# Order of the first loads and of batch 0's small steps in a windowed attention and ResMLP kernel

## Chip, cores and metric

The kernel runs on one core of a Trainium2 chip. The metric is the device time of one execution in microseconds (us). An execution has five engines: TensorE (PE, matmuls), VectorE (DVE), ScalarE (ACT), GpSimd (POOL) and SyncE (SP, which here only issues DMAs). Each works through its own instructions in the order in which they are given.

## The reference

Two stages in a row, with B = 4 batches, H = 8 heads, S = 768 positions, D = 64, d_model = H x D = 512 and d_ff = 2048:

```python
scores = q @ k.T / sqrt(D)                       # per batch and head
keep = (pos_k < 4) | ((pos_q - pos_k >= 0) & (pos_q - pos_k < 128))
a = softmax(where(keep, scores, -1e9))           # 4 sink keys and a window of 128
x = concat_heads(a @ v)                          # (B, S, 512)

a1 = alpha1 * x + beta1                          # ResMLP, affine in place of a norm
u = x + lam * (w_tok @ a1)                       # mixes the 768 positions
a2 = alpha2 * u + beta2
out = u + lam * (relu(a2 @ w_ch1) @ w_ch2)
```

Inputs and the output are float32; the matmuls of the kernel work in float16 with float32 sums.

## The kernel before

Positions are cut in six blocks of 128 rows. For a pair of heads (hp 0 to 3) and t = 0 (q) or 1 (k), `load_qk` fetches a tile, `trans` turns it with six or twelve PE transposes against the identity `iden` (L509, L512) and copies the result from PSUM to `qkT` (the evacuation, task name `ev`). For each key block j, `scores` (L617, L622), or for the first half of the heads of batch 0 `scores_by_pair` (L683, L686), makes scores in PSUM, ACT takes the exponential into `E`, and masking is done either by adding a bias tile with a matmul (`bias0`, `biasn`, L617, L683) or by a multiplication afterwards (`mk`). `sinks` and `fill_vs` handle the four sink keys (`ks`, `vs`, with the selector `sel` and the block mask `bm`). `pv` multiplies with v (L716, L723); DVE divides by the sums (L748, L749) into `x`; `half` (L758) forms the scaled copy `xh` on POOL. `tok` (L854) mixes positions with `wtokT`, the transposed w_tok, whose rows `cast_wtok` casts and transposes (L814). `uTp` (L895) transposes u, `mlp1` (L934) and `mlp2` or `prod` (L1119, L1051) are the channel MLP.

In batch 0 the first pair of heads is loaded as float32 from SyncE (`nat`, L402) and cast to float16 by DVE (L157). The six tiles of the other pairs are cast on the way by loads that GpSimd asks for (`CASTING`, L395, tile `n`). SyncE also asks for v (L429, twelve pieces), w_tok (L440, six row blocks), then for w_ch2 (`load_w`, L449) and the later batches. GpSimd asks for w_ch1 in four quarters (L453), which the 16 units fi of `mlp1` need in fours: fi 0 to 3 the first, fi 12 to 15 the fourth. Small DMAs (`gate`, L460) make SyncE wait until a quarter has landed before it asks for more.

Every step is a task, numbered in the order of the calls of `add`. `emit` writes the tasks out by four tables: `ORDER` (the order of all, and so of each engine), `ENGINES` (which engine does task i), `HOMES` (which physical buffer each tile has) and `IDLES`: (i, home, n) puts n matmuls of 128 x 128 on zeros ahead of task i on PE. These fillers (L148) keep PE occupied; nothing reads them.

A tile in the home of an earlier tile waits for that one's last reader. In before, q's float16 tile follows w_tok's first block in one `n16` home, and the last casting load takes the `nat` home of k's float32 tile. The masks (`make_masks`, L338 to L346), the selector (`make_sel`, L370, with the small identity `iden8`), the block mask (`make_bm`, L359) and `iden` (`make_iden`, L330) are made on POOL out of tiles that DVE has filled; `make_bias` (L353) makes the bias tiles of the masks on DVE.

## Time and profile before

| | |
|---|---|
| time, median of 3 runs | 255.96 us (254.75 to 256.95) |
| profiled execution, its own time | 255.43 us |
| span of its instructions | 253.2 us |
| PE busy | 245.4 us (97%) |
| DVE busy | 190.7 us (75%) |
| ACT busy | 133.3 us (53%) |
| POOL busy | 102.2 us (40%) |
| PE's clock granted | 1.00 throughout |
| DMA moved | 38.79 MB |

The span runs from the first to the last instruction; the profiled execution took 2.2 us more than its span. Busy times are sums over an engine's instructions. Times in the timelines count from the span's start. The name out<-in says which tile an instruction writes and which it reads, with the numbers of the buffers left out.

### The profile page before, as it was taken

To read this page: it belongs to the slowest core of one execution; us is meant where nothing else is said; L and a number is where in the kernel's file an instruction comes from. 1 tells how busy PE (TensorE), PEld (TensorE's weight loads), DVE (VectorE), ACT (ScalarE), POOL (GpSimd) and SP (SyncE) were. 2 spreads that over 40 slices of the span, in tenths; PEclk is the share of its full clock that TensorE was granted. 3 is DMA by queue.
4 is the path that set the end of the run, shared out by engine and by line. 5 is a ranking of instruction groups with operands and counts; after the bars stand their busy time and mean duration, and the time that the engine had idled before them with its cause. 6 is when DMAs were issued, how large, how long until landed. Compare 5 with 4: busy or idle time off the path is not lost.

```text
span 253.2 us, 5499 instructions
## 1 busy us (share of the span) xinstructions
PE 245.4 (97%) x2167; PEld 159.8 (63%) x2167; DVE 190.7 (75%) x402; ACT 133.3 (53%) x219; POOL 102.2 (40%) x124
## 2 busy tenths in 40 slices
PE   8699999999999999999999999999999999999993
PEld 7555646676545544566687686567677676667882
DVE  5588987877788874978879986577778983228892
ACT  2499925879976034787932535566660235543000
POOL 8317854895247417525682040065562220000010
PEclk9999999999999999999999999999999999999999
DMA  6999999999979998997485674420000140100317
GB/s 170 207 240 292 229 276 311 330 362 285 221 130 250 247 194 158 192 244 168 107 176 117 114 151 124 132 66 0 3 0 3 38 83 7 41 0 3 122 70 268
DMA packets 86129, 38.79 MB, mean 153 GB/s; under 512 B 73540, under 2 KB 80460, under 8 KB 86104
## 3 DMA queue, kind: packets, MB, share of 16 engines
q1 hardware_dynamic: 66576, 28.06, 46.9%
q10 hardware_dynamic: 15784, 7.11, 11.9%
q0 software_dynamic: 3744, 3.28, 8.3%
q8 instruction: 17, 0.28, 0.5%
q14 instruction: 8, 0.07, 0.1%
HBM read 29.91 MB, written 6.29 MB: 143 GB/s over the span
## 4 chain that ended last, share of the span: by engine, by line
PE 94%; DMA 3%; DVE 0%; SPq 0%; issue 0%
PE h L934 33%; PE P L1051 22%; PE tok L854 12%; PE ch L1119 8%; PE pv L723 5%; PE S L622 4%; DMA nat<-in_k_dram 3%; PE S L617 2%; PE tp L512 1%; PE pv L716 1%; PE tp L509 1%; PE wT L814 1%; PE sk L554 1%; PE idle L148 1%; PE uTp L895 1%; PE pv L609 1%
## 5 line engine op out<-in xcount | busy, mean ns | idle before, releaser
L934 PE MATMUL h<-uT,w1f 128*128 128x384 f16 x512 | 89.6, 327 | 0.0
L934 PEld LDWEIGHTS <-w1f 128*128 128x128 f16 x512 | 48.2, 98 | 31.0 <-issue 1.7
L940 ACT ACTIVATE hT<-h 128x384 f16<-128x384 f32 x77 | 37.0, 491 | 38.0 <-PE h L934 37.9
L1051 PEld LDWEIGHTS <-hT 128*128 128x128 f16 x408 | 39.4, 98 | 6.8 <-issue 0.2
L942 DVE TENSOR_SCALAR hT<-h 128x384 f16<-128x384 f32 x51 | 27.8, 555 | 20.3 <-PE h L934 19.6
L644 ACT ACTIVATE E<-S 128x1024 f16<-128x1024 f32 (+1 forms) x39 | 38.1, 1002 | 8.1 <-PE S L622 6.6
L767 POOL TENSOR_TENSOR tm<-x,la_b 128x512 f32<-128x512 f32 x18 | 24.3, 1350 | 25.2 <-DVE x L749 13.4
L854 PE MATMUL tok<-xh,wtokT 128*128 128x512 f16 x144 | 33.0, 379 | 0.0
L1064 DVE TENSOR_TENSOR x<-x,P 128x256 f32<-128x256 f32 x45 | 18.3, 419 | 11.3 <-PE P L1051 10.2
L1051 PE MATMUL P<-w2f,hT 128*128 128x256 f16 x216 | 26.5, 273 | 0.0
L854 PEld LDWEIGHTS <-wtokT 128*128 128x128 f16 x144 | 13.9, 98 | 15.0
L1119 PE MATMUL ch<-w2f,hT 128*128 128x512 f16 x96 | 23.2, 380 | 0.0
L1051 PE MATMUL P<-w2s,hT 128*128 128x256 f16 x192 | 23.1, 273 | 0.0
L1087 POOL TENSOR_TENSOR x<-x,pt 128x256 f32<-128x256 f32 x4 | 3.4, 855 | 47.5 <-DVE pt L1082 47.5
L155 ACT CAST u<-x 128x512 f16<-128x512 f32 x15 | 9.2, 615 | 24.9 <-DVE x L861 24.3
L749 DVE TENSOR_TENSOR x<-pv,rec 128x256 f32<-128x256 f32 x48 | 20.4, 425 | 1.7
L155 ACT CAST n<-nat 128x768 f16<-128x768 f32 x21 | 16.9, 828 | 7.4 <-DVE x L1130 6.3
L723 PEld LDWEIGHTS <-E 128*128 128x128 f16 x328 | 14.8, 97 | 5.0 <-issue 1.3
L861 DVE TENSOR_TENSOR x<-x,tok 128x512 f32<-128x512 f32 x24 | 16.0, 683 | 2.4 <-PE tok L854 2.3
L723 PE MATMUL pv<-vfs,E 128*128 128x65 f16 x328 | 17.6, 194 | 0.0
L584 POOL TENSOR_SCALAR_AFFINE_SELECT E<-E 128x512 f16<-128x512 f16 x12 | 7.5, 646 | 21.1 <-ACT E L644 21.1
L748 DVE RECIPROCAL rec<-pv 128x4 f32<-128x4 f32 x48 | 8.6, 179 | 7.7 <-PE pv L723 7.1
(134 smaller groups left out, 339.9 us busy)
## 6 DMA issues: line engine op xcount, KB each, us to landing
wst_w<-in_moe_w_ch_dram SPq DMA_DIRECT2D x8, 512.0 KB, 8.3
nat<-in_q_dram SPq DMA_DIRECT2D x10, 384.0 KB, 4.1
vnat<-in_v_dram SPq DMA_DIRECT2D x14, 256.0 KB, 5.4
nat<-in_k_dram SPq DMA_DIRECT2D x8, 384.0 KB, 6.6
out_dram<-x SPq DMA_DIRECT2D x11, 256.0 KB, 3.1
out_dram<-x ACTq DMA_DIRECT2D x10, 256.0 KB, 3.8
wtn<-in_moe_w_tok_dram SPq DMA_DIRECT2D x6, 384.0 KB, 4.5
w1f<-in_moe_w_ch_dram POOLq DMA_DIRECT2D x4, 512.0 KB, 14.0
```

Source lines behind the costliest of these rows:

```text
L155: nc.scalar.copy(o, i)
L644: nc.scalar.activation(eT.t, pS.t[:, :, 0 : n * w].rearrange("p e (i w) -> p e i w", i=n), AF.Exp, scale=scale)
L723: nc.tensor.matmul(po.t[:, hl, :], eT.t[:, e_, off + i, c : c + P], vf[j][:, h, :], start=(r < 2 and n == 0), stop=(n == len(parts) - 1 an ...
L749: nc.vector.tensor_mul(bx.t[:, 4 * G : 4 * G + 4, :], po.t[:, :, 0:D], rec.t.to_broadcast([P, 4, D]))
L767: engine[e].tensor_mul(bt.t, bx.t.rearrange("p h d -> p (h d)"), la1_b)
L854: nc.tensor.matmul(pt.t, wtokT[:, si, ti * P : (ti + 1) * P], hs[si].t, start=(si == 0), stop=(si == NR - 1))
L934: nc.tensor.matmul(ph.t, w1f[:, c, fi * P : (fi + 1) * P], bu.t[:, c, chk * NTOK : (chk + 1) * NTOK], start=(c == 0), stop=(c == NC - 1))
L940: nc.scalar.activation(bh.t[:, fi, :], ph.t, AF.Relu)
L942: nc.vector.tensor_scalar_max(bh.t[:, fi, :], ph.t, 0.0)
L1051: nc.tensor.matmul(pc.t, hh[:, nt * P : (nt + 1) * P], w(fi), start=(first and n_ == 0), stop=(n_ == HF - 1), skip_group_check=True)
L1064: nc.vector.tensor_add(row(bx)[:, cols], row(bx)[:, cols], pc.t)
L1119: nc.tensor.matmul(pc.t, bh.t[:, fi, nt * P : (nt + 1) * P], w2f[:, fi, :], start=(fi == 0), stop=(fi == NF - 1))
```

## The change

Only the four tables change. Of the first instructions of each engine, before and after (numbers are tasks):

| engine | before | after |
|---|---|---|
| SP | w_tok block 0 (26), q (6), k (7), then v | q (6), k (7), w_tok block 0 (26), then v; all the rest as before |
| POOL | casting load (9), sel and iden8 (5), loads 8 and 15, masks (1), load 12, bm (3), iden (0), loads 14 and 13, v casts 63 and 65, xh product 115, w_ch1 (32 to 35), xh products | sel and iden8 (5), bm (3), loads 9, 8, 15, 12, iden (0), masks (1), loads 14 and 13, a1 product (39), v cast 65, xh products 115, 118, 130, 127, v cast 66, w_ch1 (32 to 35), xh products |
| DVE | cast of w_tok block 0 (72), vs (4), make_bias (2), q cast (45), k cast (48), a1 (39, 40), b1 (41), ... | vs (4), q cast (45), k cast (48), make_bias (2), evacuation of k (50), b1 (41, 42), evacuation 54, ... |
| ACT | w_tok's evacuation (74), evacuations of q (47) and k (50), exp (91), ... | evacuation of q (47), cast of w_tok block 0 (72), exps (91, 104), evacuation 52, ... |
| PE | 65 fillers, w_tok block 0 (73), 12 fillers, q (46), 1 filler, k (49), 53, 10 fillers, scores 90, 95, ... | 67 fillers, q (46), k (49), 25 fillers, scores 90, 103, transposes 53, 51, scores 95, w_tok block 0 (73), ... |

Tasks 53 and 51 are the transposes of the second pair's k and q, whose loads are 9 and 8. On PE the first `mlp1` units are fi 1, 11, 8, 4, 10, 5 before and 11, 1, 8, 4, 10, 5 after; then, before, one `uTp`, fi 15, the other `uTp`; after, both `uTp` and then fi 15. Later on PE only neighbours change places.

28 of 1143 tasks change their engine, nearly all in batches 0 and 1 (evacuations, casts of w_tok and v, a few of relu and u). Homes: the eight q and k tiles of batch 0 now have eight `nat` homes of their own, q's `n16` home comes ahead of w_tok's block, the two v tiles of heads 4 to 7 have `wst` homes 0 and 1 (before 1 and 3), so that w_ch2's first tile (home 3) no longer follows one of them.

```diff
     ORDER = (
-        26, 6, 9, 7, 10, 5, 11, 8, 18, 15, 72, 19, 1, 12, 3, 0, 4, 2, 22, 14, 73, 74, 45,
-        48, 46, 17, 39, 49, 47, 53, 13, 40, 50, 41, 90, 95, 43, 91, 51, 54, 103, 52, 16, 44,
+        6, 7, 5, 26, 10, 3, 11, 9, 18, 8, 19, 4, 22, 15, 17, 45, 12, 48, 0, 1, 46, 49, 16,
+        28, 14, 2, 50, 47, 13, 72, 21, 39, 41, 90, 103, 20, 91, 42, 53, 104, 51, 54, 24, 95,
...
     HOMES = (
-        "471305760131011000102123203130202001333101040201500112130053316501813134100210a010022031"
+        "145602370010122001202310203211210302203140101100511203013044205121821000203331a501103130"
...
     IDLES = (
-        (73, 0, 65), (46, 0, 12), (49, 1, 1), (90, 3, 10), (61, 3, 2), (109, 3, 3), (92, 3,
-        1), (166, 1, 4), (162, 0, 1),
+        (46, 0, 67), (90, 1, 25), (166, 1, 4), (162, 0, 1),
     )
```

## The prediction

> **What bounds the kernel now.** I read the page's slices first, then the chain of waits in order of time, then the timelines of GpSimd (POOL), VectorE (DVE) and TensorE (PE) over the first 46 us, and last the tile view of `w1f`.

> From the page, three engines in 40 slices of 6.3 us:

> ```profile
> PE   8699999999999999999999999999999999999993
> ...
> POOL 8317854895247417525682040065562220000010
> ...
> DMA  6999999999979998997485674420000140100317
> ```

> PE is full from the third slice to the last. No other engine is. The DMA engines are full for the first eleven slices, so what is asked for first lands first. The chain of waits, its beginning (start, duration, what):

> ```profile
> 1.72 7.97 DMA nat<-in_k_dram
> ...
> 9.71 0.57 DVE n L157
> ...
> 10.33 0.51 PE tp L512 x6
> 10.84 0.46 PE tp L509 x12
> 11.30 0.67 PE idle L148 x10
> 11.96 0.33 PE S L686 x4
> ```

> From 10.33 the chain runs almost wholly through PE, to 248.97; one DVE add and the last store follow. So the end is 10.33 plus PE's work, and what stands ahead of it is the load of batch 0's first k: issued at 1.72, landed at 9.69, cast, transposed. PE also runs fillers (L148, matmuls nobody reads): 77 before its first transpose of q, 22 after it. From 11.96 on, eleven of them are in the stream.

> POOL and DVE, in time (start, duration, engine, operation, idle before and its releaser):

> ```profile
> 2.31 0.54 POOL L370 TENSOR_SCALAR_AFFINE_SELECT sel<-sel 128x128 f16<-128x128 f16 x1
> ...
> 5.42 0.39 POOL L346 TENSOR_SCALAR_AFFINE_SELECT mask<-mask 128x256 f16<-128x256 f16 x1
> ...
> 7.22 0.30 POOL L331 TENSOR_SCALAR_AFFINE_SELECT iden<-iden 128x128 f16<-128x128 f16 x1
> ...
> 10.58 0.71 POOL L395 DMA_DIRECT2D n<-in_k_dram  x1 [2.40 <-DVE n L157]
> ...
> 21.32 3.04 POOL L453 DMA_DIRECT2D w1f<-in_moe_w_ch_dram  x4
> ```

> ```profile
> 7.12 0.22 DVE L353 TENSOR_SCALAR bias<-mask 128x256 f16<-128x256 f16 x1
> 7.25 0.35 DVE L353 TENSOR_SCALAR biasn<-maskn 128x256 f16<-128x256 f16 x1
> 8.11 0.56 DVE L157 CAST n<-nat 128x768 f16<-128x768 f32 x1 [0.51 <-PE wT L814]
> 9.71 0.56 DVE L157 CAST n<-nat 128x768 f16<-128x768 f32 x1 [1.05 <-DMA nat<-in_k_dram]
> ```

> Three things to see: the identity is ready only at 7.52; q, landed at 5.33, is cast at 8.11 because its n16 buffer was the one of w_tok's first block (released by wT); the sixth casting load waits 2.40 for k's cast, since it shares k's nat buffer.

> Last, the place with least slack later, the tile view of `w1f` and PE's timeline:

> ```profile
> L453 POOL DMA_DIRECT2D w1f<-in_moe_w_ch_dram x4: 747/765/812, 21.3 to 23.6; - x4
> DMA to landing us min/median/max: 8.6/14.0/20.9
> ```

> ```profile
> 44.30 0.50 PE L895 MATMUL uTp<-iden,u 128*128 128x128 f16 x6
> 44.63 0.81 PE L934 MATMUL h<-uT,w1f 128*128 128x384 f16 x4
> ```

> The fourth quarter of w_ch1 lands at 23.59 + 20.92 = 44.5, and its first reader (fi 15) starts at 44.63 to 44.80. It has a margin of 0.3.

> [...] q took 4.1 from issue to landing, k, asked for 0.45 later and overlapped by GpSimd's loads, 8.0. [...] one late operand holds everything behind it, as both 8.11 and 10.58 show. [...] The granted clock is 1.00 in every window here, and PE's longest gap is 1.37 (6.20 to 7.57); the new order makes none longer. [...]

> **The change, part by part.**

> *SyncE's queue.* q takes w_tok's slot (issued 0.81, landed 3.2 later: 4.0), k takes q's (1.27 + 4.1 = 5.3, against 9.69). GpSimd's casting loads, the other traffic, start about 1.7 later, so these slots should be no slower. w_tok's block follows; its transposes sit eighth on PE now, at about 11.5. No buffer holds the casts: q at 4.1 to 4.7, k at 5.3 to 5.9. That is 4.4 gained on the data, but it is no longer the latest.

> *GpSimd.* sel needs DVE's memset (ends 1.76) and starts at 1.85 instead of 2.31. By before's start-to-start steps: sel 0.49, its small identity 0.14, bm 0.50, so 3.0; four DMA issues (0.90, 0.75, 0.72, 0.72 in before) to 6.1; identity 0.55, ready at 6.6; masks 1.40 (4.41 to 5.81 in before), ready at 8.0, 2.2 later than before; fifth and sixth load at 8.0 and 8.7, no longer at 7.47 and 10.58. [...] I take 0.2.

> *What is late next.* 67 fillers at 5.15/65 each end at 6.4; the q and k transposes run from 6.7 to 7.6. ACT evacuates q (0.80). k's evacuation goes to DVE, behind make_bias, which waits for the masks: 8.2 [...], bias 0.48, copy 0.96, ready at 9.6. The 25 fillers (0.067 each, 1.7) lie inside this wait and cost nothing. First scores at 9.7 against 11.96.

> *PE's ledger.* Before: 248.97 - 11.96 = 237.0. Leave out 11 fillers (0.74); add the first GpSimd head's transposes (0.46), w_tok's first transposes (0.34, formerly under the wait for k) and 5 fillers (0.33): 237.4. With no wait PE ends at 9.7 + 237.4 = 247.1, a gain of 1.9.

> *Waits that appear.* The second casting load (landed 11.25 in before) is wanted at 9.7 + 0.17 + 0.66 + 0.46 = 11.0. Its issue ends 1.0 later, but q and k no longer share the engines with it: estimated landing 10.6 to 11.6, cost 0 to 0.6, taken 0.2. S of block 4 needs both new evacuations (ACT after two exps, DVE after the b1 fold): 0.2. Later casting loads were 1.0 to 1.9 early in before and are wanted 1.3 to 1.7 earlier: nothing if landings stay. DVE gains about 1.2 of work net from 10 to 32 and had some 2.6 idle there: hidden. ACT loses some. Sum: 1.9 - 0.4 = 1.5.

> *w_ch1.* Its loads move on POOL from behind one xh product to behind four (0.73 each) and a v cast (0.9): by the norms that feed them, issued at about 22.6 instead of 21.3. PE meanwhile wants fi 15 at 44.8 - 1.5 + 0.34 (both uTp now stand ahead) = 43.6. In before nothing of the SyncE queue moved from 26 to 30 because w_ch2's first load waited for the v cast on its buffer; now it doesn't wait and shares from the start. The bytes ahead of the fourth quarter are the same and the engines full, so I take 43.0 to 44.5 for its landing: 0 to 0.9, taken 0. The remaining engine swaps exchange equals beside a full PE: nothing.

> Profiled execution: 255.43 (span 253.2, 2.2 around it) less 1.5 is 253.9. That run lies 0.5 under the median of the runs shown; on the median's scale 255.96 - 1.5 = 254.5.

> **Rivals.** (1) *No wait takes its place.* For it: DMA slots seen, no buffer left shared, 2.6 of DVE idle. [...] 0.72 an issue put the masks at 7.7, first scores at 9.2: ledger gain 2.4, and run scatter of 0.3 or a wait of before that modelled matmul ends hid does the rest: 253.2. Against it: DVE's order is rigid. (2) *The casting loads inherit their later issue.* If the second lands 1.6 later, 12.9, PE waits 1.9 at its transposes, where 0.2 is in the sum: the gain of 1.5 is gone, 256.2. Against it: the first six loads are bound by bandwidth, not issue. (3) *w_ch1 comes late, and the end is slower.* Place: fi 15 on PE. Break-even is a landing at 44.80 + 0.34 = 45.1, 0.6 later than before; each us beyond is one lost. If the landing moves with the issue (1.3) it is 45.8, slower by 0.7; if POOL is also held by the third v block of heads 4 to 7 (landed 20.7 in before) until 23.8, they are issued at 24.7, the last lands at 48, and the run takes 258.8. [...]

> **How the numbers follow.** Forecast 0.37 (254.5, its own range 253.4 to 255.5); rival 1 0.33; rival 2 0.12; rival 3 0.18. One per cent, 2.6 us, is about what a measurement here can tell from no change. Faster by more: rival 1 and 0.05 of the forecast, 0.38. Slower by more: rival 3 and a little of 2, 0.19. Within: 0.43. The range takes in rival 1 and the lighter half of rival 3: 252.6 to 257.8.

> **What would show it.** Right: k cast by 6.0; identity at 6.6 and masks near 8; k's evacuation on DVE starting right after make_bias; first scores at 9.2 to 9.8; 25 fillers ended before that; PE without a gap over 0.5 up to 44; fi 15 at 43 to 44. Wrong: k landing after 7, PE idle at L509 (rival 2), POOL idle ahead of w1f or PE idle at L934 (rival 3), first scores before 9.

## The result, and the profile after

| | before | after |
|---|---|---|
| time, median of 4 runs each | 255.91 us (254.75 to 256.95) | 264.34 us (263.91 to 264.55) |
| profiled execution, its own time | 255.43 us | 264.17 us |
| span | 253.2 us | 261.9 us |
| mean granted clock of PE | 1.000 | 0.985 |

The ratio after to before is 1.0328, 95% interval 1.0282 to 1.0375: slower by 8.4 us, where 1.5 us of gain were forecast. In after's profile every line number is one lower than in before's.

The page of after, the same slices as before:

```profile
PE   8799991999999999999999999999999999999993
...
POOL 7627900694996652625669004043745040000010
PEclk9999997799999999999999999999999999999999
DMA  6999999949995999799763955601000051100217
```

One slice of PE, the seventh (39.3 to 45.8), is nearly empty, and the granted clock falls in that slice and the next. Before had neither. The chain of waits in order of time (start, duration, what) has a DMA in that place:

```profile
31.34 3.47 PE tok L853 x16
38.06 6.21 DMA nat<-in_q_dram
46.17 5.45 PE h L933 x24
```

A load of batch 1's q ends the wait of batch 0's MLP, which doesn't read it. (`uT` is u transposed, taken out of PSUM and scaled by ACT and DVE; these are the "uT scalings" below, and the first `mlp1` matmul, h, reads them.) The waits from 38 to 50 us (who waited for whom: us in total, times, longest) lead there step by step:

```profile
DVE uT L879 <- ACT uT L877: 7.1, 1, 7.1
ACT uT L877 <- DMA nat<-in_q_dram: 7.0, 1, 7.0
PE h L933 <- DVE uT L879: 6.1, 1, 6.1
```

The timeline of the same place (start, duration, engine; the suffix q marks an engine's issuing of DMAs):

```profile
36.66 0.80 SPq L459 DMA_DIRECT2D gates<-w1f  x1
36.76 1.22 ACT L155 CAST u<-x 128x512 f16<-128x512 f32 x2 [0.64 <-DVE x L860]
...
38.06 0.40 SPq L401 DMA_DIRECT2D nat<-in_q_dram  x1
...
41.29 3.45 ACTq L401 DMA_DIRECT2D nat<-in_k_dram  x2
44.94 1.23 ACT L877 ACTIVATE uT<-uTp,ab 128x384 f16<-128x384 f16 x2 [6.97 <-DMA nat<-in_q_dram]
...
45.65 1.04 DVE L879 TENSOR_SCALAR uT<-uTp,ab 128x384 f16<-128x384 f16 x2 [7.11 <-ACT uT L877]
46.17 4.14 PE L933 MATMUL h<-uT,w1f 128*128 128x384 f16 x16 [6.06 <-DVE uT L879]
```

ACT in before, at the same place:

```profile
37.44 0.41 ACTq L402 DMA_DIRECT2D nat<-in_k_dram  x1
39.11 1.38 ACT L878 ACTIVATE uT<-uTp,ab 128x384 f16<-128x384 f16 x2 [1.11 <-PE uTp L895]
...
41.80 0.40 ACTq L402 DMA_DIRECT2D nat<-in_k_dram  x1
```

In after, ACT ends its casts of u at 37.98. Next in its order are two DMA issues, tasks 177 and 171 (batch 1's k of head pairs 3 and 0), and only then the scalings of uT. In before's order 177 stood behind the first cast of u and was issued at 37.44 without a wait; 171 stood behind the scalings, a relu and a cast of u and was issued at 41.80. By the trace's semaphore events, SP's and ACT's 140 transfers share eight semaphores, in before as in after, and none of the 132 issues that follow another transfer on their semaphore went out before that one had landed (the nearest 0.02 us behind it). Which transfer gets which differs from build to build: in before, the last users of 177's and 171's had landed 2.5 and 5.5 us ahead of the issues. In after, 177's semaphore was last used by gate 1 (SP, issued 36.66, landed 41.21) and 171's by the load of nat_3_0 (SP, issued 38.06, landed 44.27). So ACT stands still from 37.98 to 41.29 and from 41.75 to 44.35, with the scalings behind it; DVE's half of uT waits for ACT's; and PE idles from 40.11 to 46.17. Below, "the hold" is this standstill of ACT.

Behind the idleness the granted clock falls to 0.50 (columns: stretch and its length, busy time of PE, PEld, DVE, ACT and POOL, granted clock, DMA share, GB/s):

```profile
38.80:42.20 3.40, 1.31 (x7) 0.49 (x5) 0.00 (x0) 0.00 (x0) 0.00 (x0) 1.00 1.15 308
42.20:45.60 3.40, 0.00 (x0) 0.00 (x0) 0.00 (x0) 0.66 (x2) 0.00 (x0) 0.50 1.12 337
45.60:49.00 3.40, 2.83 (x9) 1.28 (x9) 2.76 (x5) 0.59 (x3) 0.73 (x2) 0.50 1.06 375
```

PE works from 46.17 to 49.02 at half clock, which is 1.4 us of lost work: its offset (below) grows from 5.77 to 7.15 there.

I follow the loss through the run by PE's offset: the start of a matmul in after less that of the same matmul in before, each in its one profiled execution. It is -0.79 at the first tok, -0.45 at the end of tok, +5.77 at the first h, +7.15 at the 21st h matmul, +7.65 behind the first pv of batch 1, +8.4 at P of batch 1, and +8.7 at the end.

The head, from POOL's, DVE's and PE's timeline of after:

```profile
5.15 0.59 DVE L157 CAST n<-nat 128x768 f16<-128x768 f32 x1 [0.66 <-DMA nat<-in_k_dram]
...
7.98 0.72 POOL L394 DMA_DIRECT2D n<-in_q_dram  x1
8.06 0.23 DVE L352 TENSOR_SCALAR bias<-mask 128x256 f16<-128x256 f16 x1 [2.32 <-POOL mask L345]
8.20 1.31 DVE L352 TENSOR_SCALAR biasn<-maskn 128x256 f16<-128x256 f16 x1
8.69 0.72 POOL L394 DMA_DIRECT2D n<-in_k_dram  x1
9.43 0.94 DVE L157 COPY qkT<-tp 128x768 f16<-128x768 f16 x1
10.43 0.28 PE L685 MATMUL S<-qkT 64*128 64x256 f16 x2 [1.40 <-DVE qkT L157]
```

It went nearly as forecast: k cast by 5.74, masks at 8.03, the evacuation of k right behind make_bias. One item is new: the second bias took 1.31 us, against 0.35 in before, and ended at 9.51, just behind GpSimd's two issues (9.41).

### The profile page after: what moved, and what is told of

Read it like the earlier page. It is cut to its first block, busy times and chain, and to the rows that moved or that the text cites. A ratio compares the mean times of both kernels' runs of the same rounds, so it can differ in the third digit from the quotient of the medians.

```text
span 261.9 us, 5508 instructions
## 1 busy us (share of the span) xinstructions
PE 247.4 (94%) x2165; PEld 160.6 (61%) x2165; DVE 196.9 (75%) x403; ACT 131.9 (50%) x215; POOL 111.5 (43%) x127
## 4 chain that ended last, share of the span: by engine, by line
PE 79%; DVE 6%; POOL 6%; DMA 4%; issue 2%; ACT 0%; ACTq 0%; DVEq 0%; POOLq 0%; SPq 0%
PE h L933 29%; PE P L1050 20%; PE tok L853 10%; PE ch L1118 8%; PE pv L722 4%; PE S L621 3%; DMA nat<-in_q_dram 2%; DMA lb_b<-in_moe_beta_dram 2%; POOL E L583 2%; POOL w2f L835 2%; DVE qkT L157 1%; POOL vfs L157 1%; PE S L616 1%; PE wT L813 1%; POOL xh L757 1%
## 5 line engine op out<-in xcount | busy, mean ns | idle before, releaser
L933 PE MATMUL h<-uT,w1f 128*128 128x384 f16 x512 | 90.8, 330 | 6.2 <-DVE uT L879 6.1
L933 PEld LDWEIGHTS <-w1f 128*128 128x128 f16 x512 | 48.6, 98 | 39.1 <-issue 9.8
L939 ACT ACTIVATE hT<-h 128x384 f16<-128x384 f32 x76 | 36.3, 491 | 40.9 <-PE h L933 40.6
L941 DVE TENSOR_SCALAR hT<-h 128x384 f16<-128x384 f32 x52 | 28.3, 553 | 20.9 <-PE h L933 20.4
L1050 PEld LDWEIGHTS <-hT 128*128 128x128 f16 x408 | 39.3, 98 | 6.6 <-issue 0.2
L766 POOL TENSOR_TENSOR tm<-x,la_b 128x512 f32<-128x512 f32 x18 | 25.2, 1400 | 20.4 <-DVE x L748 11.3
L155 ACT CAST n<-nat 128x768 f16<-128x768 f32 x20 | 16.2, 828 | 8.6 <-DMA nat<-in_q_dram 4.3
L860 DVE TENSOR_TENSOR x<-x,tok 128x512 f32<-128x512 f32 x24 | 16.0, 681 | 3.0 <-PE tok L853 2.8
L583 POOL TENSOR_SCALAR_AFFINE_SELECT E<-E 128x512 f16<-128x512 f16 x12 | 9.1, 788 | 16.7 <-ACT E L643 16.7
L157 POOL CAST u<-x 128x512 f16<-128x512 f32 x8 | 4.9, 614 | 25.3 <-DVE x L860 25.3
## 6 DMA issues: line engine op xcount, KB each, us to landing
w1f<-in_moe_w_ch_dram POOLq DMA_DIRECT2D x4, 512.0 KB, 12.9
```

Source lines behind the costliest of these rows:

```text
L155: nc.scalar.copy(o, i)
L766: engine[e].tensor_mul(bt.t, bx.t.rearrange("p h d -> p (h d)"), la1_b)
L933: nc.tensor.matmul(ph.t, w1f[:, c, fi * P : (fi + 1) * P], bu.t[:, c, chk * NTOK : (chk + 1) * NTOK], start=(c == 0), stop=(c == NC - 1))
L939: nc.scalar.activation(bh.t[:, fi, :], ph.t, AF.Relu)
L941: nc.vector.tensor_scalar_max(bh.t[:, fi, :], ph.t, 0.0)
L1050: nc.tensor.matmul(pc.t, hh[:, nt * P : (nt + 1) * P], w(fi), start=(first and n_ == 0), stop=(n_ == HF - 1), skip_group_check=True)
```

## The experiments

**Theories.** Theory 1: ACT's queue was held by the two issues, for want of free semaphores, and the idle PE then lost clock. Theory 2: the w_ch1 loads, asked for at 23.8 instead of 21.3, delay gate 1 and what follows (the mechanism of rival 3). Theory 3: the engine swaps behind the first MLP are the larger part. Ratios below are to the kernel before on the same chip, with 95% intervals. The edits of the tables are shown in short, with places left out (...) or as the rule by which the new ORDER was made; where two orders are joined, engines and buffers go with the steps. In ENGINES, 0 is ACT, 1 DVE, 3 POOL and 4 SP.

**1. ACT's two issues back behind their old neighbours.** 177 is in its old place, directly behind the first cast of u; 171 is behind the scalings again, but one relu (258) later than in before.

```diff
-        ... 219, 211, 204, 215, 226, 212, 175, 230, 216, 177, 220, 171, 227, ... 277, 258, 231, ...
+        ... 219, 177, 211, 204, 215, 226, 212, 175, 230, 216, 220, 227, ... 277, 258, 171, 231, ...
```

> The changed kernel with ScalarE's two transfers of batch 1 put back to the places they had before: nat_3_1 directly behind the first cast of u (where its semaphore's last user landed at 32.6), nat_0_1 behind the relu of fi 4. Everything else is as changed. Theory 1 (ScalarE's queue was held by the two issues ahead of the uT scalings, and the idle TensorE then lost its clock): the 6.06 us wait ahead of h goes to under 0.6, the 1.38 us of the halved clock go with it, and a later hold of ScalarE may return up to 1: 256.9 us, between 256 and 258. Theory 2 (the w_ch1 loads, asked for 2.5 us later, deliver late whatever ScalarE does): the wait ahead of h stays, 263 to 265. Theory 3 (the engine swaps after 60 us are the larger part): at most 2 us come back.

Measured: 1.028 (1.0244 to 1.0317). The wait ahead of the first h is gone (offset -0.37 there), but the time hardly moved. The timeline of this run shows where it went:

```profile
45.92 0.39 ACTq L401 DMA_DIRECT2D nat<-in_k_dram  x1
46.73 0.62 ACT L155 CAST u<-x 128x512 f16<-128x512 f32 x1 [2.85 <-DVE w2f L835]
...
47.41 0.79 PE L894 MATMUL uTp<-iden,u 128*128 128x128 f16 x11 [2.69 <-ACT u L155]
```

In this build 171 got the semaphore of SP's load vnat_1 (a v tile of batch 1, landed at 45.90), and was issued only at 45.92. Behind it now stood a cast of u, and PE waited 2.69 us for that at the next transposes. (The view names a cast of w2f, which the cast of u doesn't read; the x that it reads was written by 41.85.) So the expectation missed on the size: the hold is moved, not removed.

**2. Only task 171 moved back**, behind the relu 258; 177 stays ahead of the scalings.

```diff
-        ... 177, 220, 171, 227, ... 277, 258, 231, ...
+        ... 177, 220, 227, ... 277, 258, 171, 231, ...
```

> The changed kernel with only the second of ScalarE's two transfers (nat_0_1) moved behind the relu of fi 4; nat_3_1 stays ahead of the uT scalings, and its semaphore still waits for gate 1, which landed at 41.21. Theory 1: ScalarE is released at 41.8 rather than 44.8, so h starts at 43.1 and the wait ahead of it is 3.0 rather than 6.1. If the clock falls after some 2 us of idle TensorE as it did at 42.19, the halved stretch stays (some 1.4 us): 261.2; if 3 us are too short for that, 259.8. Theory 2: the wait ahead of h stays at 6, 263 to 265.

Measured: 1.0218 (1.0169 to 1.0267). Gate 1 landed earlier in the profiled run, 177 was issued at 39.72, and the wait ahead of h was 1.44; two more waits (0.48 and 0.19) followed. The size lies near theory 1's 261.2 (ratio 1.021), but partly by luck: the wait was half of the 3.0 taken. The clock stayed up in the profiled execution (258.8 us, mean 0.999) and not in the other three (260.8 to 261.2 us, mean 0.990).

**3. The same transfers, issued by SP.**

```diff
-    ENGINES[171], ENGINES[177] = "0", "0"
+    ENGINES[171], ENGINES[177] = "4", "4"
```

> The changed kernel with the same two transfers at the same place of the order, issued by SyncE rather than by ScalarE. Theory 1: ScalarE scales uT as soon as TensorE has transposed, h starts at 40.1 to 40.8 with a wait under 0.7, the clock stays at 1.00, and 7.4 us come back: 256.9, between 256 and 258. If it was the data of the two transfers, or the transfers' traffic, that held uT, nothing changes: 263 to 265. Theory 2: likewise 263 to 265.

Measured: 1.0135 (1.0094 to 1.0176). The data and their place in the order are the same, but ACT is free and PE goes through:

```profile
38.46 1.23 ACT L877 ACTIVATE uT<-uTp,ab 128x384 f16<-128x384 f16 x2 [0.60 <-PE uTp L894]
...
39.17 1.03 DVE L879 TENSOR_SCALAR uT<-uTp,ab 128x384 f16<-128x384 f16 x2 [0.73 <-ACT uT L877]
39.84 1.46 PE L933 MATMUL h<-uT,w1f 128*128 128x384 f16 x8
```

Theory 2 falls as the cause of the 6 us: the w_ch1 loads stand where after has them. The time came back by 4.9 us rather than 7.4, so something else costs about 3. The profiled execution was the fastest of the four (257.07 us; the others 258.70 to 259.00, at a clock of 0.996 or more).

**4. The w_ch1 loads moved up, ACT's issues left.** They go out from 19.41, earlier even than before's 21.32.

```diff
-        ... 115, 29, 128, ... 120, 32, 146, 84, 141, 133, 33, 147, 70, 134, 85, 34, 79, 71, 144, 86, 35, ...
+        ... 115, 32, 33, 34, 35, 29, 128, ... 120, 146, 84, 141, 133, 147, 70, 134, 85, 79, 71, 144, 86, ...
```

> The changed kernel with the four w_ch1 loads of GpSimd moved back up in its order, to about 21.5 us where they were before the change; ScalarE's two issues stay ahead of the uT scalings, and now wait for nat_3_0 and vnat_1 on SyncE, which are issued some 2 us earlier than in the changed kernel because gate 1 is. Theory 1: ScalarE stays held until these have landed (44.3 and 45.4 in the changed kernel, so 42 to 45.5 here), h starts between 43.5 and 47, and the clock falls again: 261 to 265. Theory 2 (the late w_ch1 loads are the cause): the wait ahead of h goes below 1 us, 256 to 258.

Measured: 1.0378 (1.0326 to 1.043). ACT is held as before, now until vnat_1 (SP) landed at 43.44:

```profile
42.39 1.52 ACTq L401 DMA_DIRECT2D nat<-in_k_dram  x2
44.11 1.23 ACT L877 ACTIVATE uT<-uTp,ab 128x384 f16<-128x384 f16 x2 [4.88 <-DMA vnat<-in_v_dram]
...
45.35 1.76 PE L933 MATMUL h<-uT,w1f 128*128 128x384 f16 x8 [3.98 <-DVE uT L879]
```

PE's wait is 2.1 shorter, but PE loses 1.55 at a pv at 23.8, and tok starts 1.3 later than in after. Theory 2's part is the time at which a hold ends, not the hold.

**5. The head with free semaphores.** ORDER takes after's first 210 tasks and before's rest, with their engines; ACT's two issues still stand ahead of the scalings.

```diff
-    ORDER = after
+    ORDER = after[:210] + before[210:]
```

> The first 210 steps of the changed kernel's order (all that is issued up to about 44 us, with the changed engines, both of ScalarE's transfers still directly ahead of the uT scalings), followed by the order and the engines of the kernel before. In this build the two transfers got other semaphores: their last users are the load of lam_b and a w_ch2 load that landed at 32.6, not gate 1 and nat_3_0. Theory 1 in its narrow form (it is the busy semaphores that hold ScalarE, not the place of the issues): both issues are done by 39.2, h waits under 1 us, the clock stays, and with the later steps as before the time is that of the kernel before less the head's gain of 0.5 to 0.9: ratio 0.996 to 1.001. In its wide form (issues ahead of the scalings cost as such), and by theory 2 (late w_ch1 loads): a wait of 4 to 6 us ahead of h, ratio 1.02 to 1.03. If the head itself costs something that the stall has hidden, 1.005 to 1.015.

Measured: 1.009 (1.0056 to 1.0125). Both issues go out by 38.4, before the transposes end:

```profile
37.45 0.92 ACTq L401 DMA_DIRECT2D nat<-in_k_dram  x2
...
38.61 1.23 ACT L877 ACTIVATE uT<-uTp,ab 128x384 f16<-128x384 f16 x2 [0.60 <-PE uTp L894]
...
39.99 1.46 PE L933 MATMUL h<-uT,w1f 128*128 128x384 f16 x8
```

This is the narrow form of theory 1: same place, other semaphores (last used by SP's transfers that landed by 32.57), no wait. What the run loses is one wait of 2.83 us at 58.7, at the transposes of a k of batch 1 whose load came late: in this splice SP issued nothing from 42.9 to 50.5. Until then its offset was +0.16.

**6. The later steps alone.** Before's first 244 tasks, then after's.

```diff
-    ORDER = after
+    ORDER = before[:244] + after[244:]
```

> The other half: the first 244 steps as in the kernel before, and the changed order and engines only behind them (from about 50 us on, a w_ch2 cast moved to GpSimd among them). Theory 1 with theory 3 as its remainder: what TensorE lost behind the first MLP in the changed kernel (0.50 at the first pv, 0.77 up to the second batch's P, 0.28 after that) is lost here too, 1.5 us: ratio 1.006. If the whole remainder of the run with the transfers on SyncE (ratio 1.0135) sits here: 1.013. If these steps cost nothing: 1.000.

Measured: 1.0061 (1.0036 to 1.0087), as expected of theory 3 as a remainder. The waits of PE from 60 to 140 us in this run:

```profile
PE P L1050 <- DVE hS L991: 0.5, 1, 0.5
PE pv L722 <- POOL vfs L157: 0.5, 1, 0.5
PE S L621 <- DMA qkT<-n: 0.3, 1, 0.3
```

This profile is of an execution of 258.24 us, over the median of 256.87, so its waits are examples and not a ledger of the 1.6 us.

**7. One of these steps.** Before, with the w_ch2 cast 194 moved from DVE to POOL.

```diff
-    ENGINES[194] = "1"
+    ENGINES[194] = "3"
```

> The kernel before with a single cast of w_ch2 (half of the piece with index 2) moved from VectorE to GpSimd, as in the changed kernel; nothing else. If it is GpSimd's load between 60 and 76 us that makes the first pv of the second batch wait for its cast of v (0.34 and 0.5 in the runs): the wait of 0.3 to 0.5 appears here, ratio 1.002. If not: no wait, 1.000.

Measured: 0.9984 (0.9958 to 1.0011), and no wait of PE between 60 and 80 us. That cast alone doesn't do it; which of the later swaps makes the two waits stays open.

**8. Fillers in the idle stretch.** After, with 88 fillers ahead of its first h (task 279).

```diff
-        (46, 0, 67), (90, 1, 25), (166, 1, 4), (162, 0, 1),
+        (46, 0, 67), (90, 1, 25), (166, 1, 4), (162, 0, 1), (279, 1, 88),
```

> The changed kernel with 88 more filler matmuls (of 67 ns, some 5.9 us, on a PSUM buffer that is free) ahead of the first h, where TensorE idled for 6.06 us. The transfers and ScalarE's hold stay as they are, so h starts at 46.2 as before. If the halved clock from 42.2 to 49.0 came from the idle TensorE: the clock is 1.00 throughout and 1.4 us come back, 262.9, with the offset to the kernel before at 5.8 rather than 7.15 behind the first MLP. If the clock has another cause (power of the other engines, a fixed time): 264.3.

Measured: 263.13 us, 1.0309 (1.0266 to 1.0352), clock 1.00 in the profiled run. So the idle PE was the cause of the halved clock. But the time isn't told apart from after's: in the profiled execution two waits that DVE had worked off during the slow stretch came back (0.46 at x, L860, and 0.35 at uT, L879), and the offset behind the first MLP is 7.06 against 7.15. There the 1.4 us of lost clock were nearly all cover for other waits.

**9. The hold by itself.** Two kernels that differ in one thing: after's first 244 tasks and before's rest, with 171 and 177 issued by SP (c2_no_tail_sp) or by ACT (c6_hold_no_tail).

```diff
-    ORDER = after
+    ORDER = after[:244] + before[244:]
```

> The first 244 steps of the changed kernel, with ScalarE's two transfers issued by SyncE, and from there on (about 50 us) the order and the engines of the kernel before. By the runs so far: 1.0135 with the transfers on SyncE less 1.0061 for the later steps alone gives 1.0075. If the small steps from 11 to 50 us cost nothing of themselves: 0.998 (the front's gain of 0.8 less 0.3). If the late w_ch1 loads and the transfers behind gate 2 hold TensorE later than 40 us, the ratio is 1.005 to 1.01 and a wait for a cast of batch 1's q or k, or for w1f, shows between 41 and 62 us.

> The run with the changed steps up to 50 us and the kernel before's order behind them, but with the two transfers issued by ScalarE again, as in the changed kernel; the one difference to that run is who issues them. Their semaphores are those of the changed kernel (gate 1's and nat_3_0's). Theory 1: the price of the hold by itself is what this run is above that one (1.0024). With 6.06 us of wait and the halved clock it is about 6.2: ratio 1.027, which is also the changed kernel's 1.0328 less the later steps' 1.0061. If the changed kernel's loss needed the later steps too, it stays under 1.015.

Measured: 1.0024 (1.0006 to 1.0041) with SP, 1.0265 (1.0222 to 1.0309) with ACT. The hold, with what it costs in clock, makes 0.0241, or 6.1 us. Without it, in the profile, then with it:

```profile
38.70 1.23 ACT L877 ACTIVATE uT<-uTp,ab 128x384 f16<-128x384 f16 x2 [0.59 <-PE uTp L894]
...
40.08 1.46 PE L933 MATMUL h<-uT,w1f 128*128 128x384 f16 x8
```

```profile
40.22 3.24 ACTq L401 DMA_DIRECT2D nat<-in_k_dram  x2
43.66 1.23 ACT L877 ACTIVATE uT<-uTp,ab 128x384 f16<-128x384 f16 x2 [5.80 <-DMA nat<-in_q_dram]
...
44.90 1.44 PE L933 MATMUL h<-uT,w1f 128*128 128x384 f16 x4 [4.90 <-DVE uT L879]
```

Hold 0.0241, later steps 0.0061 and remainder 0.0024 add up to 0.0326, against 0.0328 for the change; that they agree so closely is luck, since each is known to 0.002 to 0.005. The 1.0135 of run 3 lies 0.005 above what these parts give (1.0085). The intervals just allow it. Run 3's profiled execution fits the parts (257.07 us, 1.0094); what the other three lost, 1.6 us more at full clock, no trace shows.

**10. The remainder.** c2_no_tail_sp with two steps of DVE moved, then with both of its w_ch2 casts behind all scalings of the second half.

```diff
-        ... 221, 224, 225, 169, 279, 233, ... 199, 172, ... 248, 247, ...
+        ... 169, 221, 224, 225, 279, 233, ... 172, ... 248, 247, 199, ...
```

> The run with the changed steps up to 50 us, the transfers on SyncE and the later steps as before (1.0024), with two steps of VectorE moved: the last beta of x ahead of the uT scalings, into 0.73 us in which VectorE waited, and a w_ch2 cast behind the scalings of the second half's uT. If the two waits that are left ahead of h (0.41 on x at L860, 0.36 on uT at L879) are the whole remainder, 0.57 and 0.53 us of TensorE's offset go: ratio 0.998, between 0.996 and 1.000. If other waits take their place: 1.002.

Measured: 1.0037 (1.002 to 1.0055). The wait of 0.41 is gone (offset -0.46 up to 47 us), but the two casts now ran one behind the other ahead of the third scaling, and h waited 1.26:

```profile
45.49 2.60 DVE L835 TENSOR_TENSOR w2f<-wst_w,lam_b 128x512 f16<-128x512 f32 x2
48.02 0.47 DVE L879 TENSOR_SCALAR uT<-uTp,ab 128x384 f16<-128x384 f16 x1
```

> The run before with one more thing: both of VectorE's w_ch2 casts stand behind all three scalings of the second half's uT (in that run they followed each other for 2.60 us ahead of the third, and h waited 1.27 for it). If only the place of these casts made the remainder, TensorE's offset to the kernel before stays at -0.4 from the first h on and the ratio is 0.998, between 0.996 and 1.000: a gain of 0.5, the most that the changed front leaves. If the casts' delay makes another wait (for w2f, or for a relu behind them), 1.001 to 1.004.

Here 199 stands behind 242 and 181 behind 292. Measured: 0.9996 (0.9978 to 1.0013). The offset is -0.46 up to 48 us, then a wait of 0.25 for a relu on DVE (behind the first of the moved casts) takes it to -0.04. So the remainder was the order of DVE's casts against uT, and even without it no gain can be measured. No version here beats the kernel before.

**11. The front alone.** After's first 55 tasks, then the rest in before's order; in the second kernel task 50 (the evacuation of k) also stands ahead of 2 (make_bias).

```diff
-    ORDER = after
+    ORDER = after[:55] + [i for i in before if i not in after[:55]]
```

> Only the first 55 steps of the changed kernel's order (the casting loads behind selector and block mask, q and k ahead of w_tok, the steps up to the first scores at about 10.5 us, with their engines and fillers); every other step in the order and on the engine of the kernel before, so the w_ch1 loads and ScalarE's transfers are where they were. Theory 1: the front brings what it brought in the changed kernel, first scores at 10.4 and 0.7 to 0.9 us at the first tok matmul, and nothing takes it back: ratio 0.9965, between 0.995 and 0.998. Rival: the front's gain is lost by the end of the first token mixing whatever follows (vfs casts and w_tok loads come later because the queue was spent on q and k): 1.000.

> The run with the front alone, with one step moved: VectorE evacuates the first k ahead of making the two biases, since in the changed kernel the second bias took 1.31 us (0.35 in the kernel before) while GpSimd issued two casting loads, and the evacuation stood behind it. If the evacuation itself isn't held by GpSimd's issues: first scores at 9.1 rather than 10.4, the bias matmuls at 9.6 rather than 10.65, 0.8 to 1.0 us less than with the front alone: ratio 0.993. If the evacuation is held as the bias was: no change, 0.9965.

Measured: 1.0168 (1.0133 to 1.0203) and 1.0167 (1.0134 to 1.0199); both expectations missed. First scores came at 10.32 in the first, but PE then waited 2.42 us at 24.0:

```profile
PE wT L813 <- ACT es L558: 2.4, 1, 2.4
```

ACT had itself waited 2.9 for a pv before its exp at 23.99, with es two steps behind, and the clock was halved from 26.87 to 30.29. These builds mix the homes of both tables, so the wait may belong to the mixture, and they don't tell what the front is worth. In c5_casts_behind PE is 0.79 ahead at the first tok and 0.46 at the first h. But that is against one execution of before. The kernel of experiment 7, which differs from before only in a cast far behind the head, ran its head in its profiled execution so:

```profile
9.43 0.49 PE L511 MATMUL tp<-iden,n 128*128 128x128 f16 x6
...
10.98 0.39 PE L685 MATMUL S<-qkT 64*128 64x256 f16 x4
```

Its first k landed at 8.59, against 9.69 in before's profile, its first scores came 0.91 earlier, and it is 0.80 ahead at the first tok with before's own head. In experiment 6, with that head too, k landed at 8.95 and PE was 1.10 behind at the first tok. The ten profiled kernels that keep after's first 180 steps are all 0.65 to 0.90 ahead there. So the changed front is the steadier one; that it is faster on the mean, three executions of the old one don't show, and nor do the times (0.9996 in c5_casts_behind). Those show less scatter: twelve of c5_casts_behind's fourteen lie within 0.22 us, and no twelve of before's nineteen on that chip within 1.1.

In the second kernel the evacuation was not held by GpSimd's issues (0.96 as ever), but the biases came later, beside GpSimd's a1 product:

```profile
9.42 1.28 POOL L1168 TENSOR_TENSOR la_b<-la_b,lam_r 128x512 f32<-128x512 f32 x1
9.54 1.25 DVE L352 TENSOR_SCALAR bias<-mask 128x256 f16<-128x256 f16 x1
```

## Why the prediction was wrong, point by point

- **The step that failed** is the last term of the sum, "The remaining engine swaps exchange equals beside a full PE: nothing." It speaks of swaps between engines and puts everything else that moves at nothing by leaving it out. Among the moved steps were two DMA issues, 177 and 171, that stay on ACT and went ahead of the uT scalings. I priced them neither as instructions of ACT's queue nor for what they wait on; measured alone they cost 6.1 us (experiment 9). The prediction had said that one late operand holds everything behind it, and had applied that to the head alone. The new ORDER shows both, and before's trace shows ACT issuing them. Which semaphores they would get it can't show; that they can be held, and that uT stands behind them, could be asked.
- **The same term, later steps**: 1.0061, or 1.6 us, in place of nothing (experiment 6); which of them is open.
- **"PE's longest gap is 1.37 ...; the new order makes none longer"** failed with it: the gap is 6.06, and the granted clock fell to 0.50 for 6.83 us.
- **PE's ledger and the head**: first scores at 10.43 for 9.7. The term that was mis-sized is make_bias: 0.48 was taken, and it lasted 1.45 (8.06 to 9.51). Ahead of the masks the forecast had taken 0.2 (8.2 for 8.0), because DVE's casts fall among GpSimd's issues: my estimate, which no trace of before showed. The masks were ready at 8.03 and the casts took 0.59 each, against 0.56 in before. For the biases nothing was taken. With 10.43 in place of 9.7 the same sum gives a gain of 0.7, and 0.79 is what the profile has at the first tok. But the yardstick was one execution too: the 9.69 at which k landed and the 11.96 of the first scores came 0.7 to 1.1 earlier in two other executions of the same head (experiment 11), so the room for a gain at the head differs between executions by half of the forecast gain or more.
- **"What is asked for first lands first"** holds for the big loads of before's first 4 us (asked for at 0.81, 1.27, 1.31, 1.72, 2.28, 2.94 and 3.69, landed at 4.03, 5.33, 9.38, 9.69, 10.13, 11.25 and 12.62), but not between queues later: in before a w_ch2 load that SP asked for at 26.64 landed at 34.90, and GpSimd's last w_ch1 quarter, asked for at 23.59, at 44.50.
- **"Waits that appear"**: the second casting load landed at 10.62 and cost no wait, as rival 2's refutation had it.
- **w_ch1**: issued from 23.8, not about 22.6, but the fourth quarter landed at 41.90, earlier than the 43.0 to 44.5 taken and than the 44.5 of before. The judgement that the later issue need not mean a later landing held, and not because of the hold: without it, in experiment 3, the landing was at 41.81. Rival 3 named the right line, PE idle at L934 (L933 in after), though at fi 15 and not at the first h, and the right sign, but not the cause: w1f was there, as experiment 3 shows with h at 39.84 and the same loads.

## What to carry to other kernels

In these traces a DMA issue has its place among the instructions of the engine that issues it: ACT's two took 0.46 and 0.39 us, after standing 3.3 and 2.6 us until the last users of their semaphores, DMAs of SP, had landed, and the scalings stood behind them. Before moving an issue ahead of compute work, ask what it waits for and what stands behind it. Where the engine computes on the critical path, let SP issue the transfer: here this alone was worth 6.1 us. When a small gain is hoped for at the head, follow it to the first place where another engine's order sets the end; here VectorE's order around uT took 1.1 us of TensorE's offset back (-0.32 to +0.79 in c2_no_tail_sp), more than the 0.65 by which it led at the first tok. And profile the kernel before more than once: the landing that the forecast started from moved by 1.1 us between executions of the same head, where 1.5 us of gain were forecast.
